# Five small edits to the expert stage of an attention + mixture-of-experts kernel on one core

## The chip, the cores and the metric

One NeuronCore of a Trainium2 chip. The metric is device time in microseconds (us), the median of several executions. Five engines work on the core, each with an instruction queue of its own that it takes in order: PE (TensorE, matmuls; PEld are its weight loads), ACT (ScalarE), DVE (VectorE), POOL (GpSimd) and SP (SyncE, which here only starts DMAs). They meet through semaphores that a framework sets from the buffers that each instruction reads and writes.

## The reference

Attention in chunks of 64 over q, k, v of shape (2, 8, 576, 64) gives x with 1152 rows (tokens) of 512. Then a mixture of experts picks one of 8 experts for each token, and then a dense sum over 4 domains follows:

```python
expert_idx = np.argmax(x @ w_gate, axis=1)          # capacity 288 rows an expert
h = np.maximum(np.einsum('ecd,edf->ecf', disp, w1), 0.0)   # 512 -> 1024
y = np.einsum('ecf,efd->ecd', h, w2)                # 1024 -> 512
...
for e in range(E):                                  # 4 domains
    h = np.maximum(x @ w1[e], 0.0)
    out += p[:, e:e + 1] * (h @ w2[e])
```

With the given data six experts get tokens. In the order in which the kernel takes them they have 210, 288 (384 cut to the capacity), 64, 174, 192 and 128.

## The kernel before

**Stages.** Attention and routing come first (to about 57 us), then the experts one after the other (to about 227 us), then the dense stage. All products are made exact enough by splitting a number into a high and a low part: ACT writes the high part (`part_hi`, `hi_lo`'s first line), DVE the low part (`part_lo`, `hi_lo`'s second line), and PE makes three products, high x high, low x high, high x low.

**Weights.** An expert's weights lie in four raw buffers `raws[0..3]` (j = 0 and 2: first layer; 1 and 3: second layer) and their split copies `hls[0..3]`. Each is handled in two halves h: a DMA of 512 KB (`load`, SP's queue), `part_hi(j, h)`, `part_lo(j, h)`, after which the raw half is loaded again for the expert after the next (`load(k + 2, j, h)`).

**Blocks.** The rows of an expert are gathered by POOL (`gather`, line 403, from x in DRAM) into `xrs`. They are worked off in blocks: block 0 of 128 rows, block 1 of 128 more, and a small block 2 of up to 64. Which blocks an expert has is decided on the chip (`form_r`, the `If`s at lines 700, 717 and 718; the first expert has its own at 705). Here the six experts run block 1 and 0; 1, small and 0; 0; small and 0; small and 0; 0: eight blocks of 128 rows and three small ones. An engine whose `If` is not taken still has to reach it and to count its semaphore on by what the skipped block would have counted.

**In a block** (`block`, line 578) PE computes the first layer in two halves of 512 columns (`first`), ACT copies each out of PSUM (`out_of_array`), PE turns it (`turn`), ACT and DVE make high and low parts `ht` of it (lines 613 and 614), and PE adds the second layer into one PSUM tile `y` of 512 columns (`second`). The last part of `second` is made by column halves, first columns 0 to 255, then 256 to 511 (lines 643 and 644). Then ACT copies `y` to `yr` by halves (line 648), PE turns `yr` (line 651), and ACT and DVE split the result into `x2` (line 658). `tps`, `pg0`, `pg1` and `y` are PSUM tiles of one bank each. `hs` and `ht` come from a pool with two buffers for each tag; the tag "h" serves `ht` of blocks of both sizes.

**The order around it is written by hand.** `place(i)` in a block runs the list `also[i]`: while block 0 of an expert k is worked off, the next expert's rows are turned and split (`xprep`), and the halves of its weights are split as their slots come free (lines 738 to 761). The rest is left for `late`, line 661, at the beginning of the next expert: DVE's low parts of `raws[1]` and both parts of `raws[3]`, four DVE instructions in a row and two of ACT, and the DMAs behind them. The first expert has an order of its own (lines 681 to 710): `places` is eight small DVE instructions that fill in the list of experts which SP reads for its loads, and `chores` (`dense_rows`) are some 17 small ones spread over block 0.

**The end of attention.** `X[i]` (four buffers) holds 128 rows of x and is written to DRAM by SP (line 240). The first gather (line 406) reads that DRAM tensor and the index list `gidx0` (DVE, line 397).

Of the kernel before, what the change touches and what calls it, by code (L numbers as in the profile page):

```python
# [9 lines left out]
F32 = mybir.dt.float32  # L10
F32R = mybir.dt.float32r
# [9 lines left out]
P = 128  # L21
NTOK = 1152
NT = NTOK // P
# [3 lines left out]
DM = H * D  # L27
KD = DM // P
# [5 lines left out]
NF = FH // P  # L34
# [37 lines left out]
def kernel(ctx: ExitStack, tc: tile.TileContext, kqv_d, wg, w_all, dp, cst, out, cap):  # L72
    nc = tc.nc
# [45 lines left out]
    def part_lo(j, h):  # L119
        a, b = HALVES[h]  # L120
        nc.vector.tensor_tensor(out=hls[j][:, 1, a:b], in0=raws[j][:, a:b], in1=hls[j][:, 0, a:b].bitcast(F32), op=ALU.subtract)  # L121
# [5 lines left out]
    with ExitStack() as ast:  # L127
# [72 lines left out]
        S, E, ET, X, XT, LR, R, OHR, OHT, OACC = ({} for _ in range(10))  # L200
# [123 lines left out]
        for j in range(NT):  # L324
            if 1 <= j < 3:
                warm(WARM[1], "xt")
            a, b, c, d = j, j - 1, j - 2, j - 3
# [41 lines left out]
        n = NT - 1  # L369
# [20 lines left out]
        tokens(n)  # L390


        g0 = sp.tile([P, 3, NE], F32, bufs=1, name="g0")
        nc.vector.tensor_tensor(out=g0, in0=t_ps, in1=bc(oh0, 3, 1), op=ALU.mult)
        gidx0 = cp.tile([P, 3], I32, name="gidx0")
# [128 lines left out]
    with ExitStack() as est:  # L524
# [14 lines left out]
        def hi_lo(hi, lo, src):  # L539
            nc.scalar.copy(hi, src)  # L540
            nc.vector.tensor_tensor(out=lo, in0=src, in1=hi.bitcast(F32), op=ALU.subtract)  # L541
# [31 lines left out]
        def load(k, j, h):  # L573
            a, b = HALVES[h]
            src = w_all[bass.ds(regs[k], 1)] if k <= NE else w_all[k:k + 1]
            nc.sync.dma_start(out=raws[j][:, a:b], in_=src[:, j, :, a:b].rearrange("a p f -> p (a f)"))

        def block(k, w, also=()):

            lo, n = wins[w]
            both = n < P
            hs, ht = {}, {}
            pg = (pg0[w], pg1)

            def products(o, t, wt, start, stop):

                pairs = ((0, 0), (0, 1)) if both else PAIRS
                for i, (a, b) in enumerate(pairs):  # L590
                    nc.tensor.matmul(o, t(a), wt(b), start=start and i == 0, stop=stop and i == len(pairs) - 1, skip_group_check=True)  # L591

            def turned(o, a):
                if both:
                    nc.tensor.matmul(o, a, twice, start=True, stop=True)
                else:
                    nc.tensor.transpose(o, a, ident)

            def first(h, kds):
                for kd in kds:  # L600
                    products(pg[h], lambda a: xsmall[k % 2][:, kd].rearrange("p a n -> p (a n)") if both else xbig[k % 2][:, a, kd, lo:lo + n],
                             lambda b: w1(h, b, kd), kd == 0, kd == KD - 1)

            def out_of_array(h):
                hs[h] = hp_.tile([P, FH], F32, tag="hs", name="hs")
                nc.scalar.copy(hs[h], pg[h])

            def turn(h):
                tp = (tps, pg0)[h][w][:, 0:NF * n].rearrange("p (f n) -> p f n", f=NF)
                for j in range(NF):  # L610
                    turned(tp[:, j], hs[h][:, j * P:j * P + P])
                ht[h] = hp_.tile([P, NF, 2, n], F32R, tag="h", name="ht")
                nc.scalar.activation(out=ht[h][:, :, 0], in_=tp, func=ACTF.Relu)
                nc.vector.scalar_tensor_tensor(out=ht[h][:, :, 1], in0=tp, scalar=0.0, in1=ht[h][:, :, 0].bitcast(F32),  # L614
                                               op0=ALU.max, op1=ALU.subtract)

            def second(h, ffs, cols=slice(0, DM)):
                for j in ffs:
                    products(y[:, cols], lambda a: ht[h][:, j].rearrange("p a n -> p (a n)") if both else ht[h][:, j, a],
                             lambda b: w2(h, b, j)[:, cols], h == 0 and j == 0, h == NH - 1 and j == NF - 1)  # L620

            def place(i):
                for go in also[i] if also else ():
                    go()

            first(0, range(KD))
            out_of_array(0)
            place(0)
            first(1, (0, 1))
            turn(0)  # L630
            place(1)
            first(1, (2, 3))
            out_of_array(1)
            place(2)
            second(0, (0, 1))
            turn(1)
            place(3)
            second(0, (2, 3))
            place(4)

            second(1, range(NF - 2))
            halves = [slice(j * DM // 2, (j + 1) * DM // 2) for j in range(2)]
            for cols in halves:
                second(1, range(NF - 2, NF), cols)
            yr = hp_.tile([P, DM], F32, tag="ys", bufs=1, name="yr")
            ty = tps[w][:, 0:KD * n].rearrange("p (d n) -> p d n", d=KD)
            for cols in halves:
                nc.scalar.copy(yr[:, cols], y[:, cols])
            place(5)
            for d in range(KD):  # L650
                turned(ty[:, d], yr[:, d * P:d * P + P])
            at = o_r[k] + lo
            if both:
                at = nc.s_assert_within(o_r[k] + form_r[k] * P - P, 0, NTOK + 2 * P,
                                        skip_runtime_bounds_check_because="the small block is that of forms 2 and 3")
            cols = bass.ds(at, n)
            for d in (slice(0, KD // 2), slice(KD // 2, KD)) if not both else (slice(0, KD),):
                hi_lo(x2[:, 0, d, cols], x2[:, 1, d, cols], ty[:, d])
            place(6)

        def late(k):

            for h in range(2):
                part_lo(1, h)
                load(k + 1, 1, h)
            for h in range(2):
                part_hi(3, h)
                part_lo(3, h)
                load(k + 1, 3, h)

        def expert(k):
# [3 lines left out]
            if k == 0:  # L675
                with tc.manual_schedule(engines={ENG.Pool}):
                    gather(0, (2,))
                    gather(1)

                    nc.gpsimd.memset(x2[:, :, :, P:NTOK].bitcast(F32), 0.0)  # L680
                for h in range(2):
                    part_lo(0, h)
                ts = (tps[0], tps[2], pg0[0], pg1)
                for w in range(2):
                    for kd in range(KD):
                        if w == 0 and kd == KD - 1:
                            for i in range(WARM[6]):
                                nc.tensor.matmul(ts[kd], wz[:, 0:P], wz, start=True, stop=True)
                        xturn(0, kd, ts[kd], w)
                for kd in range(KD):  # L690
                    xsplit(0, kd, ts[kd])
                for j in (2, 1):
                    for h in range(2):
                        part_lo(j, h)
                chores = list(dense_rows())
            elif k + 2 < NE:
                gather(k + 2)
            if k:
                late(k)
                with tc.If(form_r[k] > 2):  # L700
                    block(k, 1)
            else:

                count(1)
                with tc.If(form_r[0] > 2) as two:
                    block(0, 1, [[], [lambda: part_lo(3, 0)], [places], [lambda: part_lo(3, 1)], [], [], []])
                with two.Else():
                    places()
                    for h in range(2):
                        part_lo(3, h)  # L710
                regs.extend(numbers(pli[0:1, :], engines=(ENG.SP,), max_val=NE + NDOM - 1))
                for j in (0, 2, 1, 3):
                    for h in range(2):
                        load(1, j, h)
                xprep_small(0, pg0[2])
                gather(2)
# [6 lines left out]
            def hi(i, j, h):  # L723
                also[i].append(lambda: part_hi(j, h))

            def lo(i, j, h):
                def go():
                    part_lo(j, h)
                    load(k + 2, j, h)
                also[i].append(go)  # L730

            def nxt(i, kd):
                if k + 1 < NE:
                    t = (pg0[1], pg0[2], tps[1], tps[2], pg1)[len(turns)]
                    turns.append(t)
                    also[i].append(lambda: xprep(k + 1, kd, t) if kd < KD else xprep_small(k + 1, t))
# [21 lines left out]
            nxt(5, 2)  # L758
            hi(4, 1, 0)
            hi(4, 1, 1)  # L760
            nxt(6, 3)
            for i in range(1, 6):
                also[i] += chores[4 * i - 4:4 * i]
# [9 lines left out]

        expert(0)
        late(NE)


# [187 lines left out]
```

## Time and profile before

| | |
|---|---|
| three runs | 607.54, 608.60, 610.81 us (median 608.6) |
| profiled execution: its time, its span | 608.95 us, 607.2 us |
| mean granted TensorE clock | 0.993 of full speed |
| busy: PE, PEld | 575.0 us (95%), 505.1 us (83%) |
| busy: DVE, ACT, POOL | 297.5 us (49%), 201.0 us (33%), 68.1 us (11%) |
| HBM | 100 GB/s over the span |

In the rows below times count from the span's start. A row of the timeline gives the start and the length of a run of like instructions, their engine and line, what they write and read, their number, and in brackets how long the engine stood idle ahead of them and what ended that idle time. "DVEq L700" means that the queue of DVE passed the branch at line 700; "issue" means that nothing in the profile explains the wait. Instructions of a run overlap, so a run of n is shorter than n times one.

### The profile page before, as it was taken

Reading aid. Unit: us, or ns where it says so; the run is one execution under the profiler, and the core shown is the slowest. Engines: PE = TensorE matmul, PEld = TensorE weight load, DVE = VectorE, ACT = ScalarE, POOL = GpSimd, SP = SyncE. Lnnn points to the kernel's source line nnn. Section 1 sums busy time; section 2 is a strip of 40 time slices with the busy share of each in tenths; the row PEclk is TensorE's granted clock in tenths of the full one; section 3 lists DMA queues with packets and bytes.
Section 4 is the critical chain, followed back from the end, with each engine's and each line's share of the span. In section 5 each row is a group of like instructions: output and inputs, shape, how many; then the busy total and the mean of one; then the engine's idle time right before and its main releaser. Section 6 shows DMA issues by size and latency. Waiting matters only on the chain.

```text
span 607.2 us, 9022 instructions
## 1 busy us (share of the span) xinstructions
PE 575.0 (95%) x3453; PEld 505.1 (83%) x3453; DVE 297.5 (49%) x584; ACT 201.0 (33%) x402; POOL 68.1 (11%) x63
## 2 busy tenths in 40 slices
PE   6998989998898989999999999999999999999995
PEld 3785767776676769999999999999999999989984
DVE  4898856157454675243453353353363363354222
ACT  4785264277363773012212211211211211211110
POOL 3321906001101140000000000000000000000032
PEclk8999999999999998999999999999999999999999
DMA  8781298138636495100120120120220000000022
GB/s 310 278 302 68 72 307 281 51 137 285 221 131 192 151 282 183 63 0 6 66 69 1 70 69 2 70 70 1 70 70 1 1 1 0 1 1 1 1 80 82
DMA packets 17324, 61.38 MB, mean 101 GB/s; under 512 B 2720, under 2 KB 2864, under 8 KB 16624
## 3 DMA queue, kind: packets, MB, share of 16 engines
q1 hardware_dynamic: 14544, 52.95, 25.3%
q0 software_dynamic: 2720, 7.66, 4.2%
q8 instruction: 34, 0.56, 0.4%
q14 instruction: 26, 0.21, 0.1%
HBM read 55.86 MB, written 4.75 MB: 100 GB/s over the span
## 4 chain that ended last, share of the span: by engine, by line
PE 60%; issue 1%; POOL 0%; POOLq 0%; DVE 0%
PE pg L811 31%; PE po L840 20%; PE po L859 8%; POOL out L504 0%; PE po L874 0%; POOLq L961 0%; DVE xr L847 0%; POOLq L915 0%; POOLq L504 0%
## 5 line engine op out<-in xcount | busy, mean ns | idle before, releaser
L811 PE MATMUL pg<-x,hl 128*128 128x384 f32 (+1 forms) x1152 | 190.1, 325 | 2.2 <-DVEq L771 2.2
L811 PEld LDWEIGHTS pg<-x,hl 128*128 128x128 f32 x1152 | 187.0, 189 | 3.6 <-issue 2.4
L840 PE MATMUL po<-hl,h 128*128 128x512 f32 (+1 forms) x588 | 134.6, 387 | 0.0
L840 PEld LDWEIGHTS po<-hl,h 128*128 128x128 f32 x588 | 108.3, 188 | 22.2
L121 DVE TENSOR_TENSOR hl<-raw,hl 128x1024 fp32r<-128x1024 f32 x80 | 95.3, 1219 | 23.1 <-ACT hl L117 21.3
L821 ACT ACTIVATE h<-pg 128x384 fp32r<-128x384 f32 x64 | 31.5, 492 | 187.8 <-PE pg L811 186.0
L822 DVE SCALAR_TENSOR_TENSOR h<-pg,h 128x384 fp32r<-128x384 f32 x64 | 35.7, 558 | 95.9 <-ACT h L821 95.9
L117 ACT CAST hl<-raw 128x1024 fp32r<-128x1024 f32 x80 | 81.6, 1058 | 2.0 <-DMA raw<-in_w_all 1.1
L591 PE MATMUL pg<-hl,xt 128*128 128x512 f32 x240 | 61.9, 402 | 6.5 <-issue 2.9
L591 PE MATMUL y<-hl,ht 128*128 128x512 f32 (+1 forms) x300 | 63.4, 357 | 4.1 <-DVE ht L614 3.9
L591 PEld LDWEIGHTS y<-hl,ht 128*128 128x128 f32 x300 | 47.4, 188 | 15.6 <-DVE ht L614 8.7
L847 DVE SCALAR_TENSOR_TENSOR xr<-po,mcol,xr 128x512 f32<-128x512 f32 (+1 forms) x43 | 31.7, 738 | 57.6 <-PE po L840 55.2
L591 PEld LDWEIGHTS pg<-hl,xt 128*128 128x128 f32 x240 | 43.2, 188 | 17.8 <-issue 6.9
L859 PE MATMUL po<-h,hl 128*128 128x288 f32 x384 | 52.5, 296 | 0.0
L859 PEld LDWEIGHTS po<-h,hl 128*128 128x128 f32 x384 | 51.9, 188 | 0.0
L818 ACT CAST h<-pg 128x288 fp32r<-128x288 f32 x32 | 12.8, 400 | 97.0 <-DVE pg L816 97.0
L403 POOL DMA_INDIRECT xr<-x_d,gidx x24 | 25.2, 1050 | 119.3 <-PEq L700 92.6
L868 POOL MEMSET raw<- 128x512 f32 x1 | 0.5, 527 | 270.6 <-DVE hl L121 270.6
L865 DVE TENSOR_TENSOR rest<-po,rest 128x288 f32<-128x288 f32 x28 | 12.8, 458 | 27.1 <-PE po L859 27.1
L816 DVE SCALAR_TENSOR_TENSOR pg<-pg,xt 128x288 f32<-128x288 f32 x32 | 22.3, 697 | 1.7 <-PE pg L811 1.7
L819 DVE TENSOR_TENSOR h<-pg,h 128x288 fp32r<-128x288 f32 x32 | 14.7, 458 | 15.4 <-ACT h L818 15.4
L541 DVE TENSOR_TENSOR x<-tp,x 128x256 f32 (+1 forms) x19 | 8.1, 425 | 25.8 <-ACT x L540 25.2
(168 smaller groups left out, 398.1 us busy)
## 6 DMA issues: line engine op xcount, KB each, us to landing
raw<-in_w_all SPq DMA_DIRECT2D x72, 512.0 KB
kqv<-in_kqv SPq DMA_DIRECT2D x8, 768.0 KB
raw<-in_w_all SPq DMA_DIRECT2D x4, 1024.0 KB
x_d<-x SPq DMA_DIRECT2D x9, 256.0 KB
xt<-meta_d SPq DMA_DIRECT2D x1, 1056.0 KB
kqv<-in_kqv SPq DMA_DIRECT2D x3, 256.0 KB
xr<-x_d,gidx POOLq DMA_INDIRECT x24
cc<-in_cst SPq DMA_DIRECT2D x1, 373.5 KB
```

What stands on the lines that cost most here:

```text
L117: nc.scalar.copy(hls[j][:, 0, a:b], raws[j][:, a:b])
L121: nc.vector.tensor_tensor(out=hls[j][:, 1, a:b], in0=raws[j][:, a:b], in1=hls[j][:, 0, a:b].bitcast(F32), op=ALU.subtract)
L403: nc.gpsimd.indirect_dma_start(out=xrs[k % 2][0:n, w, :], out_offset=None, in_=x_d[:, :], in_offset=bass.IndirectOffsetOnAxis(ap=ix, axis=0))
L591: nc.tensor.matmul(o, t(a), wt(b), start=start and i == 0, stop=stop and i == len(pairs) - 1, skip_group_check=True)
L811: nc.tensor.matmul(pg[:, 0:n], w1(u % 2, a, kd)[:, ff * P:ff * P + P], x2[:, b, kd, g * GW:g * GW + n], start=c == 0, stop=c == 3 * KD - 1)
L816: nc.vector.scalar_tensor_tensor(out=hs, in0=hs, scalar=0.0, in1=domain(u // NH), op0=ALU.max, op1=ALU.mult)
L819: nc.vector.tensor_tensor(out=h[:, ff, 1, 0:n], in0=hs, in1=h[:, ff, 0, 0:n].bitcast(F32), op=ALU.subtract)
L821: nc.scalar.activation(out=h[:, ff, 0], in_=pg[:, 0:GW], func=ACTF.Relu)
L822: nc.vector.scalar_tensor_tensor(out=h[:, ff, 1], in0=pg[:, 0:GW], scalar=0.0, in1=h[:, ff, 0].bitcast(F32), op0=ALU.max, op1=ALU.subtract)
L840: nc.tensor.matmul(po, h[:, ff, a, tt * P:tt * P + P], w2(u % 2, b, ff)[:, cols], start=c == 0, stop=c == 3 * NF - 1)
L847: nc.vector.scalar_tensor_tensor(out=acc[t][:, cols], in0=po, scalar=pe, in1=acc[t][:, cols], op0=ALU.mult, op1=ALU.add)
L859: nc.tensor.matmul(po[:, 0:W], w2(u % 2, b, ff)[:, d * P:d * P + P], h[:, ff, a, 0:W], start=c == 0, stop=c == 3 * NF - 1)
```

## The change

Four tiny POOL memsets into the last four `X` buffers are put ahead of the first gather. The `ht` buffers get a tag for each block size. In a block, each column half of `y` is copied right behind its own products. The result of a 128-row block is split into `x2` in one step, not two. `late` loses the first half of `raws[1]`: `part_lo(1, 0)` and its load now stand at place 4 of block 0 of the expert before; in the first expert `part_lo(1, 1)` is put off to place 1 of its block 1.

```diff
@@ -390,6 +390,9 @@
+        for i in range(NT - 4, NT):
+            nc.gpsimd.memset(X[i][0:1, 0:1], 0.0)
+
         g0 = sp.tile([P, 3, NE], F32, bufs=1, name="g0")
@@ -609,7 +612,7 @@
-                ht[h] = hp_.tile([P, NF, 2, n], F32R, tag="h", name="ht")
+                ht[h] = hp_.tile([P, NF, 2, n], F32R, tag=f"h{n}", name="ht")
@@ -640,12 +643,11 @@
             halves = [slice(j * DM // 2, (j + 1) * DM // 2) for j in range(2)]
+            yr = hp_.tile([P, DM], F32, tag="ys", bufs=1, name="yr")
             for cols in halves:
                 second(1, range(NF - 2, NF), cols)
-            yr = hp_.tile([P, DM], F32, tag="ys", bufs=1, name="yr")
+                nc.scalar.copy(yr[:, cols], y[:, cols])
             ty = tps[w][:, 0:KD * n].rearrange("p (d n) -> p d n", d=KD)
-            for cols in halves:
-                nc.scalar.copy(yr[:, cols], y[:, cols])
             place(5)
@@ -654,15 +656,13 @@
-            for d in (slice(0, KD // 2), slice(KD // 2, KD)) if not both else (slice(0, KD),):
-                hi_lo(x2[:, 0, d, cols], x2[:, 1, d, cols], ty[:, d])
+            hi_lo(x2[:, 0, :, cols], x2[:, 1, :, cols], ty)
             place(6)
 
         def late(k):
 
-            for h in range(2):
-                part_lo(1, h)
-                load(k + 1, 1, h)
+            part_lo(1, 1)
+            load(k + 1, 1, 1)
@@ -689,9 +689,8 @@
-                for j in (2, 1):
-                    for h in range(2):
-                        part_lo(j, h)
+                for j, h in ((2, 0), (2, 1), (1, 0)):
+                    part_lo(j, h)
@@ -703,8 +702,9 @@
-                    block(0, 1, [[], [lambda: part_lo(3, 0)], [places], [lambda: part_lo(3, 1)], [], [], []])
+                    block(0, 1, [[], [lambda: part_lo(1, 1), lambda: part_lo(3, 0)], [places], [lambda: part_lo(3, 1)], [], [], []])
                 with two.Else():
+                    part_lo(1, 1)
                     places()
@@ -758,6 +758,7 @@
             hi(4, 1, 0)
             hi(4, 1, 1)
+            lo(4, 1, 0)
```

## Rows read from the trace of the kernel before

**Rows 1.** Busy time by stretch: PE, PEld, DVE, ACT, POOL, granted clock, DMA share, GB/s.

```profile
120.00:140.00 20.00, 17.21 (x93) 13.99 (x93) 12.05 (x17) 12.97 (x22) 3.03 (x3) 1.00 0.41 140
```

**Rows 2.** The chain that ended last: start, length, work.

```profile
229.09 18.73 PE pg L811 x96
...
270.73 8.32 PE pg L811 x48
```

**Rows 3.** Timeline, 52 to 80 us: first gather and start of the first expert.

```profile
56.09 0.18 DVE L397 TENSOR_REDUCE gidx<-g 128x3 int32<-128x24 f32 x1
...
57.14 1.18 POOL L403 DMA_INDIRECT xr<-x_d,gidx  x1 [19.33 <-DVE st L420]
...
63.08 0.76 DVE L541 TENSOR_TENSOR xt<-tp,xt 128x256 fp32r<-128x256 f32 x2 [0.24 <-ACT xt L540]
63.10 0.19 PEld L591 LDWEIGHTS pg<-hl,xt 128*128 128x128 f32 x1 [0.42 <-ACT xt L540]
```

**Rows 4.** The same timeline: DVE, and PE's weight loads, in the first expert's block 1.

```profile
64.42 4.62 DVE L121 TENSOR_TENSOR hl<-raw,hl 128x1024 fp32r<-128x1024 f32 x4
...
72.23 0.69 DVE L614 SCALAR_TENSOR_TENSOR ht<-pg,ht 128x512 fp32r<-128x512 f32 x1 [0.27 <-ACT ht L613]
...
72.98 2.63 PEld L591 LDWEIGHTS y<-hl,ht 128*128 128x128 f32 x17 [0.22 <-DVE ht L614]
```

**Rows 5.** Timeline of PE and of ACT: ends of a 128-row and of a small block.

```profile
146.47 4.45 PE L591 MATMUL y<-hl,ht 128*128 128x512 f32 x24
...
151.01 0.65 ACT L648 COPY yr<-y 128x256 f32<-128x256 f32 x2 [1.05 <-PE y L591]
...
151.43 0.71 PE L597 MATMUL tp<-cc,yr 128*128 128x128 f32 x4 [0.30 <-ACT yr L648]
...
153.05 0.37 ACT L540 CAST x<-tp 128x256 f32 x1 [0.49 <-DVE x L541]
...
165.48 1.10 PE L595 MATMUL tp<-cc,yr 128*128 128x64 f32 x8 [0.52 <-ACT yr L648]
```

**Rows 6.** Groups by line (count | busy us, mean ns of one | idle before): full-width copy, half-width products.

```profile
L606 ACT COPY hs<-pg 128x512 f32<-128x512 f32 x22 | 13.0, 589 | 19.4 <-PE pg L591 18.8 <-issue 0.3 <-ACTq L700 0.3
...
L591 PE MATMUL y<-hl,ht 128*128 128x256 f32 x120 | 15.8, 279 | 0.0
```

**Rows 7.** Timeline of DVE, ACT and PE: start of the fourth expert.

```profile
154.13 4.62 DVE L121 TENSOR_TENSOR hl<-raw,hl 128x1024 fp32r<-128x1024 f32 x4
...
158.92 0.38 ACT L613 ACTIVATE ht<-tp 128x256 fp32r<-128x256 f32 x1 [2.44 <-DVEq L700]
...
155.69 1.19 PE L591 MATMUL pg<-hl,xt 128*128 128x512 f32 x4 [0.76 <-issue]
...
159.82 1.20 PE L591 MATMUL y<-hl,ht 128*128 128x512 f32 x4 [1.11 <-DVE ht L614]
```

**Rows 8.** Timeline of PE: starts of the second, the sixth and the third expert.

```profile
101.12 1.44 PE L591 MATMUL y<-hl,ht 128*128 128x512 f32 x5 [0.68 <-DVE ht L614]
...
216.24 0.44 PE L544 MATMUL pg<-cc,xr 128*128 128x128 f32 x2 [0.69 <-DVEq L700]
...
218.84 1.44 PE L591 MATMUL y<-hl,ht 128*128 128x512 f32 x5 [0.32 <-DVE ht L614]
...
138.69 3.37 PE L591 MATMUL pg<-hl,xt 128*128 128x512 f32 x14 [1.91 <-issue]
```

**Rows 9.** Timeline of DVE: place 5 of block 0, fourth expert.

```profile
180.65 0.42 DVE L541 TENSOR_TENSOR xt<-tp,xt 128x256 fp32r<-128x256 f32 x1 [1.76 <-ACT xt L540]
```

**Rows 10.** Timeline of ACT, DVE and PE, then PE by stretch with the granted clock: dense stage's start.

```profile
226.72 0.37 ACT L540 CAST x<-tp 128x256 f32 x1 [0.25 <-PE tp L597]
...
228.33 0.41 DVE L541 TENSOR_TENSOR xt<-pg,xt 128x256 fp32r<-128x256 f32 x1
...
229.09 3.12 PE L811 MATMUL pg<-x,hl 128*128 128x384 f32 x10 [2.19 <-DVEq L771]
...
230.00:231.00 1.00, 1.00 (x4) 0.50 0.01 2
```

## The prediction, made before the changed kernel was run

> **What bounds the kernel now.** I read the busy shares first: PE 95%, no other engine above half. A share is an average over three stages, so next came the table of stretches. In the expert stage PE stands idle for 2.8 of 20 us [rows 1], with ACT and DVE at six tenths each: here PE waits for others, often for a microsecond or less. The chain that ended last goes back through nothing but PE products to 229.09, the first product of the dense stage [rows 2]. So whatever lets the expert stage end earlier is worth its full size, and all five edits lie ahead of that point. Last I read the timeline engine by engine, to see which wait ends last at each place.
>
> **The change, part by part.** Signs: minus is time saved.
>
> *Gather.* The index list is ready at 56.27 (56.09 + 0.18) and the gather starts at 57.14, 0.87 later, on a POOL that had been idle for 19 us [rows 3]. The four memsets run in that idle time and take over the waits for the writes of x, so at most those 0.87 us go. Little of it arrives: DVE then has low parts of weights to finish and was free only 0.24 us before it got its first piece of the expert's rows, with PE's first product at the same moment [rows 3]. I take -0.24 (bounds 0 and -0.87).
>
> *First expert's low parts.* Four of DVE's low parts run in a row before the first `ht`; a run of four takes 4.62 us, 1.155 each [rows 4]. Taking one away there helps no one much, since PE passes that point without standing. But it returns at place 1, in front of `places` and of the second `ht`. DVE has 0.27 us idle there, and PE's weight load at 72.98 already waits for that `ht` [rows 4]. So 1.155 less the idle 0.27, less about 0.15 by which the first `ht` comes earlier: +0.72 (bounds 0 and +1.16).
>
> *Halves of the block sum.* The words of the change promise an overlap: ACT copies one half while PE works on the other. Before, the first copy should already have been free to start when its own half was done. It didn't: PE's products end at 150.92 (146.47 + 4.45) and both copies follow at 151.01 [rows 5]. Nor do two readers share such a tile: ACT's reading of the second half of `tp` stood 0.49 us until DVE had read the first [rows 5]. So waits go by the whole PSUM tile. Then the copy of the first half, now put between the two runs of products, makes PE's second run wait for it. The price is 0.09 us from PE to ACT (150.92 to 151.01), 0.37 us for a copy of 256 columns (as long as the like-sized read [rows 5]), 0.05 back (151.38 to 151.43), and the overlap of products that is lost: one takes 0.28 us, but 120 keep PE busy for 15.8, 0.13 each [rows 6]. That is 0.09 + 0.37 + 0.05 + 0.15 = +0.66 a block. Given back: the turning of `yr` begins at 151.43 [rows 5], 0.51 after the products, and takes 0.71 for four. With the first half copied long before, two go at once and only the other two wait the 0.51, ending near 0.51 + 0.40, so -0.31. In a small block four of the eight (1.10 us for all [rows 5]) go ahead: -0.47. Sum: 8 x 0.35 + 3 x 0.19 = +3.4. Bounds: if PE needn't wait, 8 x -0.31 + 3 x -0.47 = -3.9; if nothing is given back, 11 x 0.66 = +7.3. I take +3.4, since both waits by the whole tile are seen.
>
> On this the Trainium skill speaks against the change: PSUM — Partial Sum Buffer, section "PSUM bank collisions raise a hardware error", says that two engines may not be in one bank (and the same quarter of the partitions) at once, whatever columns they touch, so it has to be guarded by bank. By that rule the sum is the one forecast here; if columns alone counted it would be 7.3 us lower. The two waits in this trace agree with the rule; that PE waits for a reader of other columns no row of this trace shows.
>
> *Low part moved a block ahead.* Every expert after the first began with four low parts on DVE. In the fourth expert they run from 154.13 to 158.75; ACT's `ht` waited 2.44 us for DVE to pass the branch at line 700, and PE's second layer stood 1.11 us for DVE's `ht` [rows 7]. Now there are three, 1.155 less, and the result ahead of them is split in one step, not two, which ends 0.36 us sooner (worked out below). DVE is then free 1.5 us earlier. With a tag of its own `ht` of the small block no longer depends on the skipped block, so ACT need not wait for that branch at all. What is late next is PE itself: the second half of its first layer stood 0.76 us at 155.69 [rows 7], right when ACT was through with two splits of weights that the merged step also brings forward, by about 0.6. The 1.11 go, and some 0.5 of the 0.76: -1.6, and the same in the fifth expert. In the second expert PE stood 0.68 us, plus some 0.17 for the broken overlap of two products (one lasts 0.4, 14 in a row 3.37 [rows 8]): -0.85. In the sixth it stood 0.69 at 216.24 and 0.32 at 218.84 [rows 8], with 0.27 of broken overlap: -1.3. In the third it stood 1.91 us for nothing that the profile shows and never for DVE [rows 8]: 0. Sum: -0.85 - 1.6 - 1.6 - 1.3 = -5.35 (bounds 0 and -5.65, all of the 0.76 included).
>
> *Where it goes.* Place 4 of block 0: behind it DVE waits 1.76 us for ACT [rows 9], so 1.155 fit; if that cover went, the next expert's rows would be split later by as much, while PE needs them only a block end later. The DMA behind it, 512 KB, moves with it by some 4 us and keeps its place in SP's queue, so nothing is passed; SP waits for the same DVE instruction as before. In the first expert the small `chores` and so POOL's scatter of them come 1.2 us later, far ahead of their use. All this at 0.
>
> *Result split in one step.* From ACT's first read to the end of DVE's last low part it takes 226.72 to 228.74, 2.02 us [rows 10]. Merged: ACT 0.59 for 512 columns [rows 6], 0.05, DVE 0.69 [rows 4], then DVE's next piece, 0.33 behind a running one: 1.66. The dense stage's first product waits for exactly this chain (2.19 us, until DVE passes line 771 [rows 10]): -0.36.
>
> *Clock.* After those 2.19 us the granted clock stands at 0.50, the lower of the two levels, for over 3 us [rows 10], and 96 products take 18.73 us where 48 take 8.32 [rows 2]: 2.09 lost. The idle time shrinks to 2.19 - 0.36 = 1.83. The nearest row is the 1.91 us in the third expert, from 136.78 to 138.69 [rows 8], and the clock of that stretch was 1.00 [rows 1]. Bounds 0 and -2.09; by the nearest row I take -2.09.
>
> **Sum.** -0.24 + 0.72 + 3.4 - 5.35 - 0.36 - 2.09 = -3.9. The profiled execution took 608.95, 0.35 above the median; 608.95 - 3.9 = **605.0 us**. The clock's term may be in some of the shown runs and not in others, which spread over 3.3 us, so I don't take the 0.35 off again.
>
> **Rivals.** *The clock falls all the same:* the shortened pause is still long, and 1.91 against 2.19 is a thin margin. For it: one row at 0.50. Time: 605.0 + 2.1 = 607.1. *Something else holds PE at the expert starts:* the 0.76 and the 1.91 are unexplained ("issue"), and if such waits, or ACT's two splits, end last there, about half of the 5.35 is lost: 607.7. *The copies do overlap:* the two observed waits would then come from something other than the tile; 605.0 - 7.3 = 597.7. *Slower:* the new 0.51 us pause in the block sum stands close before the pause of the branch and the one at `yr`; if the clock falls at the ends of experts, each costs up to 2.09. The dense start then counts as before, so the base is 607.1. Two such places give 611.3, about no change; from three on (613.4) it is slower, and all five give 617.6. Against it: a pause of 1.91 at just such a place left the clock up [rows 1, 8].
>
> **How the numbers follow.** A measurement of this kernel can tell 0.5% (3.0 us) from no change, so faster means under 605.6 and slower over 611.6. Chances: forecast 0.50, clock falls all the same 0.28, something else holds PE 0.10, copies overlap 0.05, clock at the experts' ends 0.07. The forecast lies 0.6 beyond the bound of faster, so 0.32 of its 0.50 are faster; with 0.05 from the overlap and 0.03 from the clock rival that makes 0.40. Slower has the 0.07, no change the other 0.53. Range 603.0 to 608.8: below, the gather gives all 0.87 and the block sums cost 1.5 less; above, the two nearer rivals and 1.1 for the first expert's bound and the spread of runs. Left out are the overlap, the slower rival and tails, 0.2 together.
>
> **What would show it.** PE idle ahead of the last six half-width products, released by ACT's copy, 0.5 us in all eleven blocks: right on the halves; no such wait, and the sum is far too high. Three low parts, not four, at the expert starts, and PE's waits there for `ht` under 0.2 us: right on the move. PE's weight load in the first expert's block 1 waiting about 0.9 us for the second `ht`. The first dense product at 227 us or a little earlier, and the clock in the 4 us behind it at 1.00. Wrong would be waits for `ht` as before, or the lower clock between 76 and 225 us.

## The result, and the profile after

**Result.** The changed kernel takes 615.29 us (median of 10 runs, 612.72 to 618.42), the kernel before 607.89 us in the same comparison (10 runs, 605.39 to 613.43). The ratio is 1.0123, 95% interval 1.0092 to 1.0154: slower by about 7.5 us. The forecast was 605.0, its range ended at 608.8, and slower had a chance of 0.07. The prediction was wrong in size and in sign.

The profiled execution of the changed kernel took 618.39 us, one of the longest of its ten and 3.1 above their median, with a span of 616.6 us; its rows hold somewhat more loss than the median run. From its page: the engine totals, the granted clock in 40 slices, and three groups of PE (busy, mean ns | idle before, releaser).

```profile
PE 582.0 (94%) x3453; PEld 509.8 (83%) x3453; DVE 296.5 (48%) x576; ACT 200.8 (33%) x394; POOL 73.3 (12%) x67
...
PEclk8999999897999998999999999999999999999999
...
L812 PE MATMUL pg<-x,hl 128*128 128x384 f32 (+1 forms) x1152 | 189.7, 324 | 4.2 <-ACTq L772 4.2
...
L594 PE MATMUL pg<-hl,xt 128*128 128x512 f32 x240 | 65.6, 420 | 8.5 <-issue 5.5
L594 PE MATMUL y<-hl,ht 128*128 128x512 f32 (+1 forms) x300 | 65.6, 361 | 6.4 <-ACT yr L649 5.1
```

PE issues the same 3453 matmuls and is busy for 7 us longer, though no product was added: some ran at the lower clock. Ahead of the second layer's products it now stands 5.1 us for ACT's copies, ahead of the first layer's 5.5 us for "issue", and the dense stage's first product waits 4.2 us for ACT's queue at line 772, where before it waited 2.19 for DVE's [rows 10].

Where it goes is seen from PE's start of each stage in the two profiled executions:

| PE starts | before | after | later by |
|---|---|---|---|
| first product of the first expert | 63.10 | 64.57 | 1.47 |
| second expert | 94.01 | 96.10 | 2.09 |
| third | 135.60 | 140.50 | 4.90 |
| fourth | 152.81 | 161.90 | 9.09 |
| fifth | 181.59 | 189.48 | 7.89 |
| sixth | 210.34 | 217.20 | 6.86 |
| dense stage | 229.09 | 238.65 | 9.56 |

The first 1.47 is attention, whose work is unchanged but for the memsets; in the profiles of all the kernels below PE's first work for the experts starts anywhere between 58.6 and 62.1 us. The fourth and fifth experts, with the small blocks, gain 1.2 and 1.0 us. The losses sit in three places: in the second expert (2.8), in the third (4.2), and in the sixth and at its end (2.7). From the timeline of PE, the rows that end in those places, with the fourth expert's second layer and one block's half-width products:

```profile
111.11 0.44 PE L600 MATMUL tp<-cc,yr 128*128 128x128 f32 x2 [1.53 <-ACT yr L649]
...
145.18 5.51 PE L594 MATMUL pg<-hl,xt 128*128 128x512 f32 x14 [3.52 <-issue]
...
167.10 1.20 PE L594 MATMUL y<-hl,ht 128*128 128x512 f32 x4
...
172.24 0.74 PE L594 MATMUL y<-hl,ht 128*128 128x256 f32 x4 [0.52 <-ACT yr L649]
...
221.93 1.78 PE L594 MATMUL pg<-hl,xt 128*128 128x512 f32 x7 [1.96 <-issue]
...
238.65 6.63 PE L812 MATMUL pg<-x,hl 128*128 128x384 f32 x28 [4.18 <-ACTq L772]
```

The row at 167.10 has no wait, where the one before stood 1.11 [rows 7]; the 0.52 at 172.24 is the forecast price of the halves. But the 1.91 "issue" in the third expert [rows 8] has become 3.52, and the 14 products behind it take 5.51 us, not 3.37. Stretches of PE there (busy with count, granted clock, DMA share, GB/s) show why:

```profile
140.00:142.00 2.00, 1.16 (x4) 1.00 0.82 297
142.00:144.00 2.00, 0.00 (x0) 0.75 0.90 283
144.00:146.00 2.00, 0.82 (x3) 0.50 0.90 272
146.00:148.00 2.00, 2.00 (x6) 0.50 0.86 199
```

PE idles, the clock falls to the lower of its two levels, and the DMA engines are 0.8 to 0.9 busy all the while. In the kernel before they had a gap there, from 0.4 us behind PE's start of this expert:

```profile
136.00:137.00 1.00, 0.78 (x4) 1.00 0.24 78
```

The load moved ahead by `lo(4, 1, 0)` fills that gap.

### The profile page after: what moved, and what is told of

It is laid out like the page before. It is cut to its first block, busy times and chain, and to the rows that moved or that the text cites. A ratio compares the mean times of both kernels' runs of the same rounds, so it can differ in the third digit from the quotient of the medians.

```text
span 616.6 us, 9004 instructions
## 1 busy us (share of the span) xinstructions
PE 582.0 (94%) x3453; PEld 509.8 (83%) x3453; DVE 296.5 (48%) x576; ACT 200.8 (33%) x394; POOL 73.3 (12%) x67
## 4 chain that ended last, share of the span: by engine, by line
PE 59%; issue 1%; POOL 0%; POOLq 0%; DVE 0%
PE pg L812 30%; PE po L841 20%; PE po L860 8%; POOL out L507 0%; PE po L875 0%; POOLq L962 0%; DVE xr L848 0%; POOLq L916 0%; POOLq L507 0%
## 5 line engine op out<-in xcount | busy, mean ns | idle before, releaser
L594 PE MATMUL pg<-hl,xt 128*128 128x512 f32 x240 | 65.6, 420 | 8.5 <-issue 5.5
L594 PE MATMUL y<-hl,ht 128*128 128x512 f32 (+1 forms) x300 | 65.6, 361 | 6.4 <-ACT yr L649 5.1
L594 PEld LDWEIGHTS pg<-hl,xt 128*128 128x128 f32 x240 | 45.9, 199 | 20.8 <-issue 8.6
L406 POOL DMA_INDIRECT xr<-x_d,gidx x24 | 31.5, 1312 | 102.5 <-PEq L699 90.7
L609 ACT COPY hs<-pg 128x512 f32<-128x512 f32 x22 | 13.0, 589 | 30.0 <-PE pg L594 24.1
```

What stands on the lines that cost most here:

```text
L406: nc.gpsimd.indirect_dma_start(out=xrs[k % 2][0:n, w, :], out_offset=None, in_=x_d[:, :], in_offset=bass.IndirectOffsetOnAxis(ap=ix, axis=0))
```

## The experiments

**Theories.** *Traffic:* the 512 KB load, moved to place 4, runs just when an engine that has taken a branch fetches its next code, which comes later then; PE stands longer and the clock falls. *Layout:* the merged split takes ACT and DVE instructions out of each 128-row block, which shifts where an engine needs new code, so that a fetch falls into a bad place. *Halves:* the pauses for ACT's copies are most of the loss. All kernels below compute the whole reference. Ratios are to runs of the kernel before on the same chip.

**load_back.** The changed kernel, with only the moved load issued late again:

```diff
-            lo(4, 1, 0)
+            also[4].append(lambda: part_lo(1, 0))
...
             load(k + 1, 1, 1)
+            load(k + 1, 1, 0)
```

> The changed kernel, but the DMA that moved with the low part stays in the next expert: the low part of the first half of raws[1] is still made at place 4, its 512 KB load is issued behind the one of the second half, in late. The instruction lists of PE, ACT and DVE stay as in the changed kernel. Traffic theory (the moved load runs just when the engines' next instructions have to be fetched, which lengthens pauses that the profile calls issue): PE's pause in the third expert falls from 3.5 to about 1.9 us, that in the sixth from 2.0 to under 0.5, the clock stays up in the third expert, and the time falls by 5 to 9 us, to 606 to 610. Layout theory (another number of instructions per block moved the points at which code is fetched into bad places): the pauses stay within 0.5 us and the time within 1.5 us of the changed kernel. Halves theory (the pauses at the block sums and the clock behind them are all of it): within 1.5 us too.

Measured: 609.96 us, ratio 1.0003 (0.9976 to 1.0029). One DMA per expert issued later takes the whole loss away: against the 1.0123 of the changed kernel that is 7.3 us. PE's pause in the third expert is back at 1.68 and in the sixth at 0.64; the pause ahead of the dense stage stays, 4.38 for ACT's queue.

**halves_back.** The changed kernel, with both copies behind all products again:

```diff
             for cols in halves:
                 second(1, range(NF - 2, NF), cols)
-                nc.scalar.copy(yr[:, cols], y[:, cols])
...
+            for cols in halves:
+                nc.scalar.copy(yr[:, cols], y[:, cols])
```

> The changed kernel with only the copies of the block sum put back behind both halves. Halves theory: nearly all of the 7.4 us goes, 608 or less, and the clock stays up. Traffic and layout theory: the eleven pauses of 0.5 us go, some 3.4 us less and up to 3 more in the second expert, where ACT's second copy came late and the clock fell; the pauses of the third and sixth expert and at the start of the dense stage stay, so 609 to 612.

Measured: 611.19 us, 1.0033 (1.0008 to 1.0057). The pauses stay (4.33 in the third expert, 1.94 in the sixth, 4.05 ahead of the dense stage), so they do not come from the halves. Against the 1.0123 of the changed kernel the time is 0.90% (5.5 us) less, nearly twice what the copies cost by themselves (halves_alone below).

**x2_two_steps.** The changed kernel, with the split of the result in two steps again:

```diff
-            hi_lo(x2[:, 0, :, cols], x2[:, 1, :, cols], ty)
+            for d in (slice(0, KD // 2), slice(KD // 2, KD)) if not both else (slice(0, KD),):
+                hi_lo(x2[:, 0, d, cols], x2[:, 1, d, cols], ty[:, d])
```

> The changed kernel with only the split of a 128-row result put back to two steps. By itself it should cost 0.3 to 1 us. Layout theory: ACT and DVE have as many instructions in a block as before, so ACT's 3.4 us at line 772 ahead of the dense stage and its late copy in the second expert go, 3 to 5 us less than the changed kernel: 610 to 612. Traffic theory: PE's pauses stay (3.5 and 2.0 us) and the time is within 1.5 us of the changed kernel.

Measured: 614.39 us, 1.0067 (1.0044 to 1.0089). Ahead of the dense stage ACT's stall is gone (2.19, for DVE, as before); the pauses of the third and the sixth expert stay (3.88 and 1.74). So these are two causes. Against the 1.0123 it is 0.56% (3.4 us) less.

**move_alone.** The kernel before with only the low part and its load moved (and the first expert's order):

```diff
+            lo(4, 1, 0)
...
-            for h in range(2):
-                part_lo(1, h)
-                load(k + 1, 1, h)
+            part_lo(1, 1)
+            load(k + 1, 1, 1)
...
```

> The kernel before with only the low part, with its load, moved a block ahead (the first expert's order included). The forecast's step alone: -5.35 + 0.72, so 603.3 against 607.9. Traffic theory: the same gain, but PE's pauses in the third and sixth expert grow by 1.6 us each, the clock may fall behind the longer one (2.1) and at the dense start code comes some 2 us later: about 607 to 610, no gain. Layout theory: PE's pauses as in the kernel before (1.9 and 0.2), about 603 to 604.

Measured: 608.79 us, 0.9997 (0.9969 to 1.0025). The waits for `ht` are gone and the gain with them: PE stands 4.15 us in the third expert and 1.65 in the sixth. This kernel has no `ht` buffers by block size, and still ACT's first `ht` of the fourth expert no longer waits for DVE's branch (2.44 us before [rows 7]); it waits 1.33 for PE, and 1.26 in best below, which has them. So no gain of those buffers is seen. From PE's timeline:

```profile
134.41 1.17 PE L591 MATMUL pg<-hl,xt 128*128 128x512 f32 x4 [0.66 <-PEq L716]
139.73 4.97 PE L591 MATMUL pg<-hl,xt 128*128 128x512 f32 x14 [4.15 <-issue]
```

**extra_load.** The suspected cost by itself: the kernel before, with one more load into a tile that nothing reads.

```diff
             lo(4, 2, 1)
+            also[4].append(lambda: extra(k + 2))
...
+        def extra(k):
+            ...
+            nc.sync.dma_start(out=dummy, in_=src[:, 1, :, a:b].rearrange("a p f -> p (a f)"))
```

> The kernel before with one more load of 512 KB per expert, into a tile that nothing reads, issued right behind the last load of place 4, where the changed kernel has the one that it moved. Nothing else differs and no engine but SP gets an instruction. Traffic theory: the pauses named issue after 135 and 213 us grow from 1.9 and 0.2 to about 4 and 1.7, the clock falls behind the first of them, +3 to +6 us in all. Layout theory: pauses as before, within 1 us of before.

Measured: 611.69 us, 1.0045 (1.0019 to 1.0071), with these rows of PE:

```profile
139.20 4.95 PE L598 MATMUL pg<-hl,xt 128*128 128x512 f32 x14 [3.29 <-issue]
...
216.59 1.77 PE L598 MATMUL pg<-hl,xt 128*128 128x512 f32 x7 [1.36 <-issue]
```

Nothing but an order to SP and a buffer was added, and the two pauses grow by 1.4 and 1.1 us, with the clock lower behind the first. A load at that place lengthens the pauses by itself, so traffic is shown; the +2.7 us (1.2 to 4.3) lie under the 3 to 6 expected.

What PE seems to wait for is seen in the DMA view. It lists the queues that moved something in a stretch; "instruction" queues carry the engines' code. In quarter microseconds of the third expert's start, the kernel before (135.94 to 136.19), move_alone (137.23 to 137.48) and the changed kernel (142.68 to 142.93) show one such packet each (packets, MB, share):

```profile
q8 instruction: 1, 0.02, 32.7%
```

```profile
q8 instruction: 1, 0.02, 24.0%
```

```profile
q8 instruction: 1, 0.02, 24.5%
```

The share is of 16 engines over 0.25 us, so the packets themselves take 1.31, 0.96 and 0.98 us: with the load they are not slower. That q8 is PE's is inferred: its packet lies in PE's pause in every kernel. The same view gives, for six of the fourteen kernels, the quarter in which the packet starts:

| kernel | PE starts the third expert | code packet starts, quarter from | PE goes on | that quarter to PE |
|---|---|---|---|---|
| before | 135.60 | 135.94 | 138.69 | 2.75 |
| best (below) | 134.53 | 134.84 | 137.34 | 2.50 |
| load_back | 134.16 | 134.50 | 137.00 | 2.50 |
| extra_load | 134.74 | 136.70 | 139.20 | 2.50 |
| after | 140.50 | 142.68 | 145.18 | 2.50 |
| move_alone | 134.41 | 137.23 | 139.73 | 2.50 |

From the start of the packet's quarter to PE's next product it is 2.25 to 2.75 us in all fourteen. What differs is when the packet starts: 0 to 0.5 us after the start of the expert in seven kernels with no load brought forward or added, 2.0 to 3.1 in the six with one. That is the "issue" which the profile does not explain. The DMA share goes with it. In best it falls to 0.25 half a microsecond after PE's start, in move_alone it stays at 0.91 and more (first rows: best, last: move_alone):

```profile
134.53:135.03 0.50, 0.50 (x2) 1.00 0.85 320
135.03:135.53 0.50, 0.50 (x3) 1.00 0.25 98
```

```profile
134.41:135.41 1.00, 1.00 (x4) 1.00 0.91 328
135.41:136.41 1.00, 0.17 (x1) 1.00 0.97 328
136.41:137.41 1.00, 0.00 (x0) 1.00 1.04 401
```

How a busy DMA engine holds the packet back was not tried. The fourteenth, best_merged below, has its load late and still gets the packet after 1.5: something else takes part too, layout perhaps.

**halves_alone.** The kernel before with the copies by halves, as in halves_back's diff read backwards.

> The kernel before with the half-by-half copies alone; all loads of weights and both branches of the split are as before. The prediction's own term: PE stands 0.5 us for ACT's copy ahead of the last half-width products in each of eleven blocks, partly given back: +3.4 us in all, the pauses named issue after 135 and 213 us as before (1.9 and 0.2). If code layout matters too (one branch of the chain moved by some instructions), a pause at an expert's end changes by over 1 us with no load moved, and the time is up to 4 us off that.

Measured: 611.82 us, 1.0046 (1.0022 to 1.0069), +2.8 us by the ratio. The pause in the third expert is 1.35. The term stands.

**x2_alone.** The kernel before with the merged split, as in x2_two_steps's diff read backwards.

> The kernel before with the result's split merged alone. The prediction's term: -0.36 us, dense start 1.8 us after the last turn, waiting for DVE. Layout theory (the shorter program puts the place where ACT fetches its next code at the branch ahead of the dense stage): ACT stands at that branch and the first dense product waits 4 us for it though no load is moved: +1.5 to +4 us. Traffic theory (the stall needs the load that was moved): 2 us as before, time within 0.5 us of before.

Measured: 608.20 us, 1.0006 (0.9981 to 1.0031). ACT's stall is there with no load moved; who waits for what from 221 to 228 us (total, times, longest):

```profile
PE pg L810 <- ACTq L770: 3.9, 1, 3.9
ACT hl L117 <- ACTq L770: 3.5, 1, 3.5
```

So the moved load is not the cause here; whether it is layout or the merged split itself, best_merged_pad below decides. The price is made up elsewhere (the waits of 0.76 and 0.68 us in the fourth and fifth expert are gone here, while those for `ht` there grow from 1.11 to 1.38), and the time comes out the same, below the 1.5 to 4 expected.

**best.** The kernel before, with the low part moved and own `ht` buffers, the load left late as in load_back, the first expert's order, copies and split as before.

> The kernel before with the low part moved a block ahead in the second to sixth experts and with own buffers for the small block, but with the load of the weights left where it was, behind the other half's, and the first expert in its old order. If the move's cost is the traffic of the load: waits for ht at the starts of the experts gone (-3 to -5 us), pauses named issue after 135 and 213 us no more than before (about 1.9 and 0.4), 604 to 606 us against 609 for the kernel before. If the pauses come from the code's layout: a pause of 3 to 4 us after 135 us stays, time 607 to 610.

Measured: 604.26 us (602.43 to 605.80), 0.9935 (0.9911 to 0.9959): 0.65% faster than the kernel before, 1.9% faster by the two ratios than the changed one. From PE's timeline:

```profile
137.34 3.38 PE L591 MATMUL pg<-hl,xt 128*128 128x512 f32 x14 [1.64 <-issue]
154.36 1.19 PE L591 MATMUL pg<-hl,xt 128*128 128x512 f32 x4 [0.76 <-ACTq L700]
181.90 1.19 PE L591 MATMUL pg<-hl,xt 128*128 128x512 f32 x4 [0.67 <-ACTq L700]
224.24 18.46 PE L812 MATMUL pg<-x,hl 128*128 128x384 f32 x96 [2.19 <-DVEq L772]
```

No wait for `ht` of 0.6 us or more is left behind the first expert, and the third expert's pause is short.

**no_memsets.** The changed kernel without the memsets.

> The changed kernel without its four GpSimd memsets ahead of the gather; nothing else differs. The prediction's term for them was -0.24: the gather would start 0.87 us after the index list with or without them, 0 to 0.3 us slower than the changed kernel. If ACT's late copy in the second expert (2.35 us behind the products, 1.53 us of PE) belongs to the changed kernel's code, it is here again; if it was an accident of the one profiled execution, the copy comes about 1.06 us after its turn as in the three other kernels with copies by halves.

Measured: 614.40 us, 1.0085 (1.0053 to 1.0117), its interval overlapping the changed kernel's. The gather starts at 58.35, 0.84 us after the index list is ready; with the memsets it is 0.86 (57.62 to 58.48). Gathers without (first row) and with them, from POOL's timelines:

```profile
58.35 1.18 POOL L403 DMA_INDIRECT xr<-x_d,gidx  x1 [19.32 <-DVE st L420]
```

```profile
58.48 1.23 POOL L406 DMA_INDIRECT xr<-x_d,gidx  x1 [2.97 <-DVE st L423]
```

ACT's copy in the second expert, 2.35 us behind the products in the changed kernel's profile, comes after 1.06 here as in the other kernels with halves. So the 1.53 us at 111.11, and the lower clock behind it, are probably of that one execution, itself 3.1 us above the median; with one trace of the changed kernel that is not shown.

**first_alone.** The kernel before with the first expert's order alone.

```diff
-                for j in (2, 1):
-                    for h in range(2):
-                        part_lo(j, h)
+                for j, h in ((2, 0), (2, 1), (1, 0)):
+                    part_lo(j, h)
...
-                    block(0, 1, [[], [lambda: part_lo(3, 0)], [places], [lambda: part_lo(3, 1)], [], [], []])
+                    block(0, 1, [[], [lambda: part_lo(1, 1), lambda: part_lo(3, 0)], [places], [lambda: part_lo(3, 1)], [], [], []])
```

> The kernel before with one low part of the first expert moved from ahead of its rows to place 1 of its second block; no load moves. The prediction's term: +0.72 us, PE waiting 0.6 to 0.9 us for the second ht at about 73 us. Rival: the lead is eaten later, since the next block starts after a wait of its own, 0.

Measured: 608.06 us, 1.0003 (0.9977 to 1.0028). The new wait is there, 0.57 us, but the 0.72 us that PE stood for `ht` a block later (85.40 in the kernel before) is gone:

```profile
71.84 2.79 PE L591 MATMUL y<-hl,ht 128*128 128x512 f32 x17 [0.57 <-DVE ht L614]
...
83.04 1.65 PE L591 MATMUL y<-hl,ht 128*128 128x512 f32 x6
```

This run also had a pause of 1.94 in the sixth expert, with no load moved: there a late packet (2.3 us after PE's start of that expert, with the DMA engines about half busy) has other causes too.

**best_merged.** Best, with the merged split added.

> The kernel that keeps the load late, with the merged split of the result added. Layout theory: as in the kernel with that split alone, ACT stands at the branch ahead of the dense stage, the first dense product waits about 4 us, not 2.2, and the 0.7 us at the starts of the fourth and fifth experts go: 604 to 606 us. If that stall was an accident of the profiled runs: dense start after 1.8 us, 602 to 603.5.

Measured: 604.57 us, 0.9933 (0.9905 to 0.9962). The dense stage waits 3.83 us for ACT, and the 0.7 us in the fourth and fifth expert are gone, as the layout theory had it.

**best_merged_pad.** The same, with ACT's number of copies put back by one that nothing reads:

```diff
             hi_lo(x2[:, 0, :, cols], x2[:, 1, :, cols], ty)
+            if not both:
+                nc.scalar.copy(padt, wz[0:1, 0:1])
```

> The same, with one ACT copy of a single element behind each merged split of a block of 128 rows, which nothing reads: ACT's program gets its old number of copies back (the semaphore steps may differ), at some 0.2 us of an ACT that is idle there. Layout theory: the stall at the branch ahead of the dense stage goes back to about 2 us, 602 to 604. If the merged split itself (its longer ACT read, its single wait) makes the stall: 4 us as without the extra copies.

Measured: 601.86 us (600.08 to 602.18), 0.9879 (0.9849 to 0.9908): the fastest of all, and a useless ACT instruction in each 128-row block made it so (of the nine runs without it one, 601.89, is not above the highest of these six). The dense stage's first product without (first row) and with the copies:

```profile
223.39 18.46 PE L811 MATMUL pg<-x,hl 128*128 128x384 f32 x96 [3.83 <-ACTq L771]
```

```profile
222.20 18.72 PE L815 MATMUL pg<-x,hl 128*128 128x384 f32 x96 [1.66 <-DVEq L775]
```

Over all kernels the wait here is 3.8 to 4.4 us, for ACT's queue, in the six with the merged split, 2.2, for DVE's, in the seven with two steps, and 1.66, for DVE's, with the merged split and the copies. The code packets agree: in each of the six a packet of the second instruction queue, q14, starts 1.6 to 1.9 us before PE goes on, inside the stall; in the other eight no code packet starts between 4.9 and 1.1 us before. With the work of the merged split unchanged the stall is gone, so the split by itself does not make it; in the one kernel tried, the number of ACT's instructions does. The copies also moved other fetches: the third expert's pause fell from 2.75 to 1.57, the sixth's grew from 0.33 to 1.68.

## Why the prediction was wrong

- **The step that failed** is *Where it goes*, in its sentence "The DMA behind it, 512 KB, moves with it by some 4 us and keeps its place in SP's queue, so nothing is passed", costed at 0. The order of the queue was right, but what counts there is the time at which the DMA engines are busy. The load fell on the change of experts, where PE takes a branch and its next code packet has to come: the packet started 2.3 us after PE's start of the third expert, not 0.4, and the pause grew from 1.91 to 3.52 us, the clock falling in it. Between the changed kernel and load_back the load is worth 1.20% (7.3 us), between no_memsets and load_back 0.82% (5.0 us, if the memsets do nothing), between move_alone and best 0.62% (3.8 us), and as an extra load in the kernel before 0.45% (2.7 us). A wait of this kind stood in the rows read, the 1.91 "issue" [rows 8]. It was costed at 0 for the move because DVE did not end it, and nobody asked what did.
- **The low part moved a block ahead**, -5.35 with bounds 0 and -5.65: right in mechanism. Without the load's shift it is -4.0 (best, interval -5.4 to -2.5). The waits for `ht` at the experts' starts are gone. Of the 0.76 in the fourth and fifth experts, "some 0.5" was to go; in best 0.76 and 0.67 stay, for ACT's queue at line 700. With the merged split they go, as the step had said, so -5.35 was mainly too large for the move by itself. Its bound is a slip: with all of the 0.76 included the terms add up to -5.9, not -5.65.
- **Halves of the block sum**, +3.4: right, +2.8 measured (1.3 to 4.2). The pause for ACT's copy, 0.46 us once and 0.52 ten times, is there in all eleven blocks of the kernel with the copies alone: in this kernel PE does wait for a reader of other columns of the same PSUM tile. So the overlap of the first copy with the second half's products, which the change seems to promise, does not take place.
- **First expert's low parts**, +0.72: the wait came (0.57 alone, 0.56 in the changed kernel), the loss did not, +0.2 us (-1.4 to 1.7). The step stopped at the first wait and left out the one that PE already had a block later.
- **Gather**, -0.24: nothing. The wait of 0.87 us behind the index list is unchanged with the memsets done; so it is no wait that the memsets could take over. What it is stays open.
- **Result split in one step**, -0.36: the chain of ACT and DVE did get shorter (1.66 with the copies put back, against 2.19), but as written the edit left ACT waiting at the branch, where code packets come in, and the wait grew to about 4 us. No row of before showed where such a fetch falls.
- **Clock**, -2.09: not given back. Even behind a pause of 1.66 us the first 96 dense products take 18.72 us, as before [rows 2]. The row picked as nearest, a pause of 1.91 us in the third expert with the clock up, did not carry over. Only in first_alone did those 96 take clearly less, 16.89 us, behind the same 2.19. The lower clock between 76 and 225 us, named as a sign of being wrong, was there too (0.50 from 144 to 148).
- **Rivals.** The slower rival was right in that a lower clock at an expert's end would cost some 2 us (5.51 against 3.37 for 14 products), wrong in the cause: not the 0.5 us of the halves, but a pause of 3 to 4 us that the load made longer. *Something else holds PE at the expert starts*, with a chance of 0.10, pointed at the right waits, the unexplained 0.76 and 1.91, but only as gain held back (607.7); that the change could lengthen them was in no rival. *The copies do overlap* is refuted by the eleven waits.

Together, by ratios and without the load: halves +2.8, the move without its load -4.0, first expert +0.2, merged split +0.4, which makes -0.6. load_back, the changed kernel without the moved load, measured +0.2 (-1.5 to +1.8), so these agree, and the loss of 7.5 (5.6 to 9.4) goes with the load. Its price is not one number, though: 2.7 and 3.8 us beside the old copies and split, 5.0 to 7.3 in the changed kernel, where the halves (5.5) and the merged split (3.4) also cost more than alone. Taken out one at a time the three give 16 us, where the loss and the move's gain together make 11.5. The intervals of such differences are 2 to 3 us to either side, so how far the effects fail to add up, and why, stays open.

## What to carry to other kernels

Moving a load is a change of its own, even when its place in the queue stays: before costing it at nothing, look at the DMA share of the stretch into which it moves and at what else, code included, arrives there. Prices taken from one edit at a time need not add up. A pause named "issue" right behind a branch is a question to the DMA view: look for an instruction packet in it. When an edit takes instructions out of a loop body and an engine then stalls at some distant branch, try the same kernel with an idle instruction put back before blaming the edit.

## What the runs showed of the hardware

- PE's next product follows 2.25 to 2.75 us after the quarter microsecond in which a code packet of 16 KB (0.02 MB in the profile) starts, in all fourteen kernels; the packet takes 1.0 to 1.3 us of that. The whole pause in the third expert was 1.35 to 4.33 us, by how late the packet started. On this the Trainium skill, page Runtime: NRT & Kernel Launch, section "🔬 Instruction fetch mechanics", says that a sequencer refills its code in such blocks by a DMA queue of its own, that the cost of crossing into the next is "mostly hidden", but that a taken branch to code outside of what is held forces a fetch before the engine goes on. The size agrees, and the pause behind the branch fits the last, though PE still ran four products between the two. That the weights' loads make this fetch later is what the runs add.
- One ACT copy of a single element (0.18 us) per 128-row block took 2.7 us off the median (604.57 to 601.86): the stall ahead of the dense stage fell from 3.83 to 1.66 us, and with it went the code packets inside it.
- The clock is not told by the pause alone: behind 1.68 us in load_back the 14 products took 4.97 us, behind 1.64 in best 3.38. What sets it there was not tried.
